# Reordered first loads, longer warm-up, paired first tiles and four output buffers in a gated two-branch attention kernel

## Chip, cores, metric

One core of one Trainium2 chip. The metric is the device time of one execution in microseconds (us); lower is better. The kernel ran alone on its core. The granted clock is the share of TensorE's full clock that a profile shows as granted.

## The reference

Two attention branches read the same x (2048 x 1024, bf16), and a sigmoid gate mixes their outputs:

```python
q, k, v = split_heads(x @ wqkv)                 # 32 heads of 32, in each branch with its own weights
# branch A: linear attention
kv, z = einsum(phi(k), v), sum_s(phi(k))        # phi(t) = max(t,0) + min(exp(t),1) + 1e-6
a = ((phi(q) @ kv) / (phi(q) . z)) @ wo_A
# branch B: softmax over 8 keys at a dilation of 2
b = (softmax(q . k[s - 2w] * scale) @ v[s - 2w]) @ wo_B
g = sigmoid((x * gate_w).sum(-1))
return g * a + (1 - g) * b
```

## The kernel before

TensorE goes through five stages: pk (phi of branch A's keys, with the weights WkA in two column halves), G (x^T pk), the values and branch A's queries, branch B's keys and queries with its attention (eight blocks of four heads, each attended while the next is projected), and the output projection. The change touches the beginning of pk and the attention blocks.

The first loads, and the x tiles. Tiles 0 and 1 of x are transposed on TensorE from a row-major copy; the other fourteen come through transposing DMAs on the sync queue, in order, with everything else behind them.

```python
    load_rows(nc.scalar, 0, 1)
    load_rows(nc.scalar, 1, 2)
    WkA = load_w("WkA", A_wqkv, D, "wa", parts=4, only=(0,))        # four DMAs of 256 KB, sync queue
    for t in range(2, NB):
        nc.sync.dma_start_transpose(out=xT[:, :, t * P:(t + 1) * P], in_=rows(x, t * P, (t + 1) * P))
    WkA += load_w("WkA", A_wqkv, D, "wa", only=(1,))
    # ... (cut) the other rows of x, other weights
            for i in range(5):
                warm = ps_1.tile([P, 512], F32, name="warm", tag="p1")
                for j in range(4):
                    nc.tensor.matmul(warm[:, j * P:(j + 1) * P], lhsT=onesb[:], rhs=onesb[:], start=True, stop=True)
            for t in range(2):
                # ... (cut) eight 128x128 transposes of xrow into tp
                nc.vector.tensor_copy(out=xT[:, 0:4, t * P:(t + 1) * P], in_=tp[:, 0:4, :])
                nc.scalar.copy(out=xT[:, 4:8, t * P:(t + 1) * P], in_=tp[:, 4:8, :])
            for half in range(2):
                for t in range(NB):
                    # ... (cut) pj = sum over kt of xT[:, kt, tile t] x WkA[half][:, kt, :]
                    phi(pk[:, t, half * 512:(half + 1) * 512], pj)
```

The output side of an attention group. `small` has two buffers; Ob holds the normalized output until a transposing DMA has read it:

```python
                    Ob = small.tile([P, 4, 4, Dh], BF16, name="Ob", tag="Ob")
                    # ... (cut) probabilities x V into PSUM banks oB
                        nc.vector.tensor_tensor(out=Ob[:, t0:t0 + m], in0=o_[:, :, :, 0:Dh],
                                                in1=rd[:, 0:m].broadcast_to([P, m, 4, Dh]), op=ALU.mult)
                        # ... (cut)
                        nc.sync.dma_start_transpose(out=OBT[:, c, ...], in_=Ob[0:w, t0:t0 + m]...)
    # before the last block is attended:
            WoB = load_w("WoB", B_wo, 0, "wb")
            nc.sync.dma_start_transpose(out=pqT[0][:], in_=pqd[0:512, :])
```

Of the kernel before, what the change touches and what calls it, by code (L numbers as in the profile page):

```python
# [10 lines left out]
BF16 = mybir.dt.bfloat16  # L11
F32 = mybir.dt.float32
PE = mybir.EngineType.PE
DVE = mybir.EngineType.DVE
P = 128
# [26 lines left out]
def kernel(  # L42
# [11 lines left out]
    nc = tc.nc  # L54
    S, D = A_x.shape[1:]
# [9 lines left out]
    Dh = D // H  # L65
    KT = D // P
    NB = S // P
# [8 lines left out]
    wpool = ctx.enter_context(tc.tile_pool(name="wpool", bufs=2))  # L76
# [2 lines left out]
    kq = ctx.enter_context(tc.tile_pool(name="kq", bufs=2))  # L79
    ps_pj = ctx.enter_context(tc.tile_pool(name="ps_pj", bufs=2, space=bass.MemoryType.PSUM))  # L80

    def load_w(name, src, col0, tag, parts=1, only=(0, 1)):
        halves = []
        for h in only:
            w = wpool.tile([P, KT, 512], BF16, name=f"{name}{h}", tag=tag)
            c0 = col0 + h * 512
            n = KT // parts
            for i in range(parts):
                nc.sync.dma_start(
                    out=w[:, i * n:(i + 1) * n, :],  # L90
                    in_=src[i * n * P:(i + 1) * n * P, c0:c0 + 512].rearrange("(kt p) n -> p kt n", p=P))
            halves.append(w)
        return halves

    xT = big.tile([P, KT, S], BF16, name="xT", tag="xT")
    xrow = big.tile([P, NB, D], BF16, name="xrow", tag="vV")

    def load_rows(eng, t0, t1):
        eng.dma_start(out=xrow[:, t0:t1, :], in_=rows(x, t0 * P, t1 * P).rearrange("(t p) d -> p t d", p=P))

    load_rows(nc.scalar, 0, 1)
    load_rows(nc.scalar, 1, 2)
    WkA = load_w("WkA", A_wqkv, D, "wa", parts=4, only=(0,))
    for t in range(2, NB):
        nc.sync.dma_start_transpose(out=xT[:, :, t * P:(t + 1) * P], in_=rows(x, t * P, (t + 1) * P))
    WkA += load_w("WkA", A_wqkv, D, "wa", only=(1,))
# [11 lines left out]
    onesb = consts.tile([P, P], BF16, name="onesb")  # L118
# [26 lines left out]
    def phi(dst, pj):  # L145
        e = work.tile([P, 512], F32, name="e", tag="e")
        nc.scalar.activation(out=e[:], in_=pj[:], func=ACT.Exp)  # L147
        nc.vector.tensor_scalar(out=e[:], in0=e[:], scalar1=1.0, scalar2=1e-6, op0=ALU.min, op1=ALU.add)  # L148
        nc.vector.scalar_tensor_tensor(out=dst, in0=pj[:], scalar=0.0, in1=e[:], op0=ALU.max, op1=ALU.add)

    with tc.manual_schedule(engines={PE}):

        with ExitStack() as s1:
# [1 line left out]
            junk = s1.enter_context(tc.tile_pool(name="junk", bufs=1))  # L155


            for i in range(5):
                warm = ps_1.tile([P, 512], F32, name="warm", tag="p1")
                for j in range(4):  # L160
                    nc.tensor.matmul(warm[:, j * P:(j + 1) * P], lhsT=onesb[:], rhs=onesb[:], start=True, stop=True)
            for t in range(2):
                tp = ps_1.tile([P, KT, P], BF16, name="xt_ps", tag="p1")
                for kt in range(KT):
                    nc.tensor.transpose(out=tp[:, kt, :], in_=xrow[:, t, kt * P:(kt + 1) * P], identity=ident[:])
                nc.vector.tensor_copy(out=xT[:, 0:4, t * P:(t + 1) * P], in_=tp[:, 0:4, :])
                nc.scalar.copy(out=xT[:, 4:8, t * P:(t + 1) * P], in_=tp[:, 4:8, :])

            s1.enter_context(tc.manual_schedule(engines={DVE}))
            pk = big.tile([P, NB, D], BF16, name="pk", tag="pkO")  # L170
            for half in range(2):
                for t in range(NB):
                    pj = ps_1.tile([P, 512], F32, name="pk_ps", tag="p1")
                    for kt in range(KT):
                        nc.tensor.matmul(pj[:], lhsT=xT[:, kt, t * P:(t + 1) * P], rhs=WkA[half][:, kt, :],  # L175
                                         start=(kt == 0), stop=(kt == KT - 1))
                    phi(pk[:, t, half * 512:(half + 1) * 512], pj)
            zacc = junk.tile([P, D], F32, name="zacc", tag="zacc")
            gw_row = junk.tile([P, D], BF16, name="gw_row", tag="gw")
            nc.gpsimd.dma_start(out=gw_row[:], in_=gate_w.partition_broadcast(P))  # L180
            zhl = junk.tile([P, 2, D], BF16, name="zhl", tag="zhl")

            def side(t):
# [133 lines left out]
        with ExitStack() as s2:  # L317
# [31 lines left out]
            def attention_events(c, kqt, cuts, first, lag):  # L349
                GROUPS = [QT[a:b] for a, b in zip(cuts, cuts[1:])]  # L350
                state = [dict() for _ in GROUPS]
                per_bank = 2 if cuts is CUTS4 else 3

                def scores(g):
                    tiles, st = GROUPS[g], state[g]
                    W_ = sum(w for _, w, _ in tiles)
                    s4 = ps_s.tile([P, 4, 512], F32, name="s4", tag="s")
                    o = 0
                    for q0, w, k0 in tiles:
                        for i in range(4):  # L360
                            r = slice(32 * i, 32 * i + 32)
                            nc.tensor.matmul(s4[:, i, o:o + w], lhsT=kqt[r, 0, k0:k0 + P],
                                             rhs=kqt[r, 1, q0:q0 + w], start=True, stop=True)
                        o += w
                    pt = PT[count[0] % 2]
                    count[0] += 1
                    ptv = pt[:, 0:4 * W_].rearrange("p (i s) -> p i s", i=4)
                    m0 = 112 if tiles[0][1] == 128 else 0 if tiles[1][1] == 128 else 240
                    for h in range(2):
                        hs = slice(2 * h, 2 * h + 2)  # L370
                        nc.scalar.activation(out=ptv[:, hs], in_=s4[:, hs, 0:W_], func=ACT.Exp, scale=SCALE)  # L371
                        m = mask[:, m0:m0 + W_]
                        nc.vector.tensor_tensor(out=ptv[:, hs], in0=ptv[:, hs],  # L373
                                                in1=m[:, None, :].broadcast_to([P, 2, W_]), op=ALU.mult)
                    st["pt"], st["W"] = pt, W_

                def pv(g):
                    tiles, st = GROUPS[g], state[g]
                    pt, W_, n = st["pt"], st["W"], len(tiles)
                    Ob = small.tile([P, 4, 4, Dh], BF16, name="Ob", tag="Ob")  # L380
                    oB = []
                    for b in range((n + per_bank - 1) // per_bank):
                        bank = ps_o.tile([P, 512], F32, name=f"oB{b}", tag=f"o{b}")
                        m = min(per_bank, n - per_bank * b)
                        oB.append((b * per_bank, m, bank[:, 0:m * 4 * (Dh + 1)].rearrange("p (t i e) -> p t i e", t=m, i=4)))
                    for t0, m, o_ in oB:
                        for i in range(4):
                            o = sum(w for _, w, _ in tiles[:t0])
                            for tt in range(t0, t0 + m):
                                nc.tensor.matmul(o_[:, tt - t0, i, :], lhsT=pt[:, i * W_ + o:i * W_ + o + P],  # L390
                                                 rhs=V[:, cuts[g] + tt, c * 4 + i, :], start=True, stop=True)
                                o += tiles[tt][1]
                    for t0, m, o_ in oB:
                        rd = small.tile([P, 3, 4, 1], F32, name="rd", tag="rd")
                        nc.vector.reciprocal(out=rd[:, 0:m], in_=o_[:, :, :, Dh:Dh + 1])
                        nc.vector.tensor_tensor(out=Ob[:, t0:t0 + m], in0=o_[:, :, :, 0:Dh],
                                                in1=rd[:, 0:m].broadcast_to([P, m, 4, Dh]), op=ALU.mult)
                    t0 = 0
                    while t0 < n:
                        q0, w, _ = tiles[t0]  # L400
                        m = 1
                        while t0 + m < n and tiles[t0 + m][1] == w and tiles[t0 + m][0] == q0 + m * w:
                            m += 1
                        nc.sync.dma_start_transpose(
                            out=OBT[:, c, q0:q0 + m * w].rearrange("p (t s) -> p t s", t=m),
                            in_=Ob[0:w, t0:t0 + m].rearrange("p t i e -> p (t i e)"))
                        t0 += m

                ev = []
                step = 64 / len(GROUPS)  # L410
                for g in range(len(GROUPS)):
                    ev.append((first + step * g, lambda g=g: scores(g)))
                    ev.append((first + step * g + lag, lambda g=g: pv(g)))
                return ev
# [12 lines left out]
            raw = wpool.tile([P, 4, D], BF16, name="raw", tag="wc")  # L427
            fw = wpool.tile([P, 2, D], F32, name="fw", tag="wc")
            pqT = [kq.tile([P, KT, 512], BF16, name="pqT0", tag="kq")]
            nc.sync.dma_start_transpose(out=pqT[0][:], in_=pqd[0:512, :])  # L430

            def qa_keep(t, half, pj):
                nc.scalar.copy(out=raw[:, t - 12, half * 512:(half + 1) * 512], in_=pj[:])
# [90 lines left out]
```

## Time and profile before

| | before |
|---|---|
| median of the first 3 runs | 496.87 us (496.01 to 497.5) |
| span of the profiled run | 493.9 us |
| TensorE busy | 481.6 us, 98% |

The page of the profiled run: the first line gives busy time, share of the span and number of instructions of TensorE (PE); the second is the chain of work that ended last, by engine.

```profile
PE 481.6 (98%) x3276; PEld 230.1 (47%) x3336; DVE 283.4 (57%) x550; ACT 182.0 (37%) x281; POOL 8.6 (2%) x29
...
PE 96%; DMA 2%; issue 1%; DVE 0%; ACT 0%; SPq 0%; ACTq 0%; DVEq 0%
```

TensorE is the bound, so a gain can come only from its idle time or its slow time. The timeline of TensorE's matmuls in the first 40 us (start, duration, engine, line, operation, out<-in, count, and in brackets the idle time before it and what ended it):

```profile
1.13 2.32 PE L161 MATMUL warm<-onesb 128*128 128x128 bf16 x20 [1.13 <-DVE onesb L119]
4.57 1.04 PE L165 MATMUL xt_ps<-ident,xrow 128*128 128x128 bf16 x8 [1.13 <-DMA xrow<-in_A_x_dram]
5.88 1.03 PE L165 MATMUL xt_ps<-ident,xrow 128*128 128x128 bf16 x8 [0.27 <-DMA xrow<-in_A_x_dram]
6.71 28.47 PE L175 MATMUL pk_ps<-WkA_77,xT 128*128 128x512 bf16 x125
35.01 5.34 PE L175 MATMUL pk_ps<-WkA_96,xT 128*128 128x512 bf16 x24
```

TensorE waits for x tile 0 and again for tile 1. The line at 35.01 is the first matmul with WkA's second half and serves as a clock: whatever happens at the start has been settled by then. The weight loads (PEld) in front of the first projection matmuls show the rate:

```profile
6.60 0.26 PEld L175 LDWEIGHTS <-xT 128*128 128x128 bf16 x2
7.14 0.15 PEld L175 LDWEIGHTS <-xT 128*128 128x128 bf16 x1 [0.28 <-issue]
7.56 0.15 PEld L175 LDWEIGHTS <-xT 128*128 128x128 bf16 x1 [0.28 <-issue]
7.99 4.03 PEld L175 LDWEIGHTS <-xT 128*128 128x128 bf16 x19 [0.28 <-ACT xT L167]
```

Single loads at 7.14, 7.56 and 7.99 mean 0.43 us for each 512-column matmul. From 7.99 on there are 19 loads in 4.03 us, about 0.216 us each: the array has changed to its full rate. The granted clock does not show this: it reads 1.00 in every stretch of the first 14 us, so the rate at the start is read from the distance of the weight loads.

In the last attention block (the sync queue, SPq in the view, with VectorE and TensorE; three views of the same run):

```profile
359.63 4.11 SPq L430 DMA_TRANSPOSE pqT_4069<-pqd  x1
...
365.13 1.60 SPq L89 DMA_DIRECT2D WoB_4065<-in_B_wo_dram  x1
366.83 14.76 SPq L404 DMA_TRANSPOSE OBT<-Ob  x8
```

```profile
367.71 0.56 DVE L396 TENSOR_TENSOR Ob<-oB_4153,rd 128x384 bf16<-128x384 f32 x1 [2.24 <-DMA OBT<-Ob]
...
372.44 0.56 DVE L396 TENSOR_TENSOR Ob<-oB_4202,rd 128x384 bf16<-128x384 f32 x1 [3.21 <-DMA OBT<-Ob]
```

```profile
PE oB_4252 L390 <- DVE Ob L396: 1.5, 1, 1.5
...
PE oB_4202 L390 <- DVE Ob L396: 0.5, 1, 0.5
```

VectorE cannot write Ob until an output transpose two groups back has read the buffer. That transpose sits on the queue behind the transpose of pqT0 (4.11 us of issue) and a 1 MB half of WoB. VectorE waits 2.24 and 3.21 us, and TensorE, which needs the PSUM bank that VectorE has not emptied, waits 0.50 and 1.51 us.

### The profile page before, as it was taken

To read this page: it belongs to the slowest core of one execution; us is meant where nothing else is said; L and a number is where in the kernel's file an instruction comes from. 1 tells how busy PE (TensorE), PEld (TensorE's weight loads), DVE (VectorE), ACT (ScalarE), POOL (GpSimd) and SP (SyncE) were. 2 spreads that over 40 slices of the span, in tenths; PEclk is the share of its full clock that TensorE was granted. 3 is DMA by queue.
4 is the path that set the end of the run, shared out by engine and by line. 5 is a ranking of instruction groups with operands and counts; after the bars stand their busy time and mean duration, and the time that the engine had idled before them with its cause. 6 is when DMAs were issued, how large, how long until landed. Compare 5 with 4: busy or idle time off the path is not lost.

```text
span 493.9 us, 8164 instructions
## 1 busy us (share of the span) xinstructions
PE 481.6 (98%) x3276; PEld 230.1 (47%) x3336; DVE 283.4 (57%) x550; ACT 182.0 (37%) x281; POOL 8.6 (2%) x29
## 2 busy tenths in 40 slices
PE   7999999999999999999999999999998999999997
PEld 4444444446444444444444444544444444444444
DVE  2666699921329999996567676767655596000000
ACT  2333311112543333331555655565564323112121
POOL 4000000001100000000000000000000000000000
PEclk9999999999999999999999999999999999999999
DMA  8999920002422122244011141111172843110101
GB/s 232 163 317 361 345 95 0 1 0 68 152 75 70 74 88 92 94 145 139 11 33 29 27 119 38 29 28 34 31 175 54 209 86 82 36 42 33 43 33 42
DMA packets 78069, 46.03 MB, mean 93 GB/s; under 512 B 51472, under 2 KB 72080, under 8 KB 78032
## 3 DMA queue, kind: packets, MB, share of 16 engines
q1 hardware_dynamic: 77664, 44.73, 32.9%
q10 hardware_dynamic: 288, 0.52, 0.4%
q8 instruction: 26, 0.43, 0.4%
q0 software_dynamic: 80, 0.26, 0.2%
q14 instruction: 11, 0.09, 0.1%
HBM read 21.23 MB, written 7.34 MB: 58 GB/s over the span
## 4 chain that ended last, share of the span: by engine, by line
PE 96%; DMA 2%; issue 1%; DVE 0%; ACT 0%; SPq 0%; ACTq 0%; DVEq 0%
PE kq_ps L334 22%; PE d_ps L452 21%; PE pk_ps L175 11%; PE g_ps L198 11%; PE p_ps L257 11%; PE p_ps L291 8%; PE q_ps L291 1%; DMA OBT<-Ob 1%; DMA xrow<-in_A_x_dram 1%; PE kv_ps L216 1%; PE q_ps_4367 L452 1%; PE p_ps L246 1%; PE q_ps L452 1%; PE q_ps_4147 L291 0%; PE q_ps_4248 L291 0%
## 5 line engine op out<-in xcount | busy, mean ns | idle before, releaser
L198 PE MATMUL g_ps<-pk,xrow 128*128 128x512 bf16 x251 | 55.2, 379 | 0.3
L457 ACT ACTIVATE osb<-d_ps,omg 128x512 bf16<-128x512 f32 (+1 forms) x31 | 20.9, 673 | 77.0 <-PE d_ps L452 72.5
L148 DVE TENSOR_SCALAR e<-e 128x512 f32<-128x512 f32 x64 | 27.2, 425 | 36.0 <-ACT e L147 35.8
L175 PEld LDWEIGHTS <-xT 128*128 128x128 bf16 x256 | 25.3, 99 | 30.4 <-issue 0.6
L452 PEld LDWEIGHTS <-OBT 128*128 128x128 bf16 x264 | 25.8, 98 | 29.2
L198 PEld LDWEIGHTS <-xrow 128*128 128x128 bf16 x256 | 25.0, 98 | 30.2
L257 PEld LDWEIGHTS <-xT 128*128 128x128 bf16 x256 | 25.0, 98 | 30.2
L291 PEld LDWEIGHTS <-xT 128*128 128x128 bf16 x256 | 24.2, 98 | 28.0
L373 DVE TENSOR_TENSOR PT_1878<-PT_1878,mask 128x672 bf16<-128x672 bf16 (+3 forms) x42 | 23.6, 571 | 17.0 <-ACT PT_1878 L371 16.7
L334 PE MATMUL kq_ps<-xT,WqB_1861 128*128 128x512 bf16 x120 | 31.8, 379 | 1.0 <-issue 0.6
L147 ACT ACTIVATE e<-pk_ps 128x512 f32<-128x512 f32 x32 | 19.1, 597 | 36.3 <-PE pk_ps L175 35.2
L334 PE MATMUL kq_ps<-xT,WqB_1859 128*128 128x512 bf16 x124 | 31.7, 379 | 0.7 <-issue 0.5
L334 PE MATMUL kq_ps<-xT,WkB_1056 128*128 128x512 bf16 x122 | 31.6, 379 | 0.2
L340 DVE CAST kqt<-kq_ps 128x512 bf16<-128x512 f32 x32 | 22.0, 687 | 16.4 <-PE kq_ps L334 16.4
L334 PE MATMUL kq_ps<-xT,WkB_1054 128*128 128x512 bf16 x120 | 30.7, 379 | 0.4 <-issue 0.2
L373 DVE TENSOR_TENSOR PT_1879<-PT_1879,mask 128x672 bf16<-128x672 bf16 (+3 forms) x40 | 22.2, 564 | 15.3 <-ACT PT_1879 L371 15.1
L257 PE MATMUL p_ps<-WvB_112,xT 128*128 128x512 bf16 x126 | 30.6, 379 | 0.1
L257 PE MATMUL p_ps<-WvB_110,xT 128*128 128x512 bf16 x125 | 30.6, 379 | 0.1
L262 ACT CAST tmp<-p_ps 128x512 bf16<-128x512 f32 x32 | 18.8, 587 | 30.3 <-PE p_ps L257 27.9
L452 PEld LDWEIGHTS <-pqT_4425 128*128 128x128 bf16 x200 | 19.6, 98 | 22.1
L175 PE MATMUL pk_ps<-WkA_77,xT 128*128 128x512 bf16 x125 | 28.3, 386 | 0.2
L452 PE MATMUL d_ps<-WoB_4065,OBT 128*128 128x512 bf16 (+1 forms) x126 | 28.3, 366 | 0.1
(400 smaller groups left out, 669.2 us busy)
## 6 DMA issues: line engine op xcount, KB each, us to landing
out_dram<-osb SPq DMA_DIRECT2D x31, 128.0 KB, 1.9
xrow<-in_A_x_dram SPq DMA_DIRECT2D x3, 1024.0 KB, 12.0
pqd<-tmp SPq DMA_DIRECT2D x12, 256.0 KB, 2.0
V<-tmp SPq DMA_DIRECT2D x4, 264.0 KB, 2.5
WkA_77<-in_A_wqkv_dram SPq DMA_DIRECT2D x4, 256.0 KB, 5.5
WkA_96<-in_A_wqkv_dram SPq DMA_DIRECT2D x1, 1024.0 KB, 7.0
WvA_102<-in_A_wqkv_dram SPq DMA_DIRECT2D x1, 1024.0 KB, 14.3
WvA_104<-in_A_wqkv_dram SPq DMA_DIRECT2D x1, 1024.0 KB, 15.2
```

The costliest lines, as they stand in the source:

```text
L147: nc.scalar.activation(out=e[:], in_=pj[:], func=ACT.Exp)
L148: nc.vector.tensor_scalar(out=e[:], in0=e[:], scalar1=1.0, scalar2=1e-6, op0=ALU.min, op1=ALU.add)
L175: nc.tensor.matmul(pj[:], lhsT=xT[:, kt, t * P:(t + 1) * P], rhs=WkA[half][:, kt, :], start=(kt == 0), stop=(kt == KT - 1))
L198: nc.tensor.matmul(pj[:], lhsT=xrow[:, t, kt * P:(kt + 1) * P], rhs=pk[:, t, half * 512:(half + 1) * 512], start=(t == 0), stop=(t == NB - 1))
L257: nc.tensor.matmul(st["pj"][:], lhsT=xT[:, kt, t * P:(t + 1) * P], rhs=WvB[half][:, kt, :], start=(kt == 0), stop=(kt == KT - 1))
L262: nc.scalar.copy(out=v[:, half * 16:(half + 1) * 16, 0:Dh], in_=st["pj"][:].rearrange("p (h e) -> p h e", h=16))
L291: nc.tensor.matmul(st["pj"][:], lhsT=xT[:, kt, t * P:(t + 1) * P], rhs=WqA[half][:, kt, :], start=(kt == 0), stop=(kt == KT - 1))
L334: nc.tensor.matmul(st["pj"][:], lhsT=W[c // 4][:, kt, (c % 4) * P:(c % 4 + 1) * P], rhs=xT[:, kt, cols], start=(kt == 0), stop=(kt == KT - 1))
L340: nc.vector.tensor_copy(out=kqt[:, 1, cols], in_=st["pj"][:])
L373: nc.vector.tensor_tensor(out=ptv[:, hs], in0=ptv[:, hs], in1=m[:, None, :].broadcast_to([P, 2, W_]), op=ALU.mult)
L452: nc.tensor.matmul(st["ps"][:, 0:n], lhsT=lhsT, rhs=W[c0 // 512][:, c, c0 % 512:c0 % 512 + n], start=(side == 0 and c == 0), stop=(side == ...
L457: nc.scalar.activation(out=osb[:, 0:n], in_=st["ps"][:, 0:n], func=ACT.Copy, scale=omg[:, tb:tb + 1])
```

## The change

Its intent: get both x tiles to the head of two queues, let weights follow in row blocks and use each block for two tiles, keep TensorE warm until data lands, move the gate row out of the crowded start, and give the attention output four buffers, so that VectorE can run ahead of the transposes of its output. pqT0 is cut in four. The order of instructions on VectorE stays the same.

```diff
-    load_rows(nc.scalar, 0, 1)
+    load_rows(nc.sync, 0, 1)
     load_rows(nc.scalar, 1, 2)
-    WkA = load_w("WkA", A_wqkv, D, "wa", parts=4, only=(0,))
+    WkA = [wpool.tile([P, KT, 512], BF16, name="WkA0", tag="wa")]
+    for kt in range(KT):
+        (nc.scalar if kt % 2 else nc.sync).dma_start(out=WkA[0][:, kt, :], in_=A_wqkv[kt * P:(kt + 1) * P, D:D + 512])
     # ... (cut)
-            for i in range(5):
-                warm = ps_1.tile([P, 512], F32, name="warm", tag="p1")
-                for j in range(4):
-                    nc.tensor.matmul(warm[:, j * P:(j + 1) * P], lhsT=onesb[:], rhs=onesb[:], start=True, stop=True)
+            def warm_up(n): ...                 # n matmuls of 128 columns into one PSUM tile (cut)
+            warm_up(28)
             for t in range(2):                  # the TensorE transposes (cut)
+            warm_up(6)
     # ... (cut)
-                for t in range(NB):
-                    pj = ps_1.tile([P, 512], F32, name="pk_ps", tag="p1")
+                for t0, n in [(0, 2)] + [(t, 1) for t in range(2, NB)]:
+                    pj = [ps_1.tile([P, 512], F32, name="pk_ps", tag="p1") for _ in range(n)]
                     for kt in range(KT):        # each weight block for all n tiles, then the next (cut)
     # ... (cut)
-            nc.gpsimd.dma_start(out=gw_row[:], in_=gate_w.partition_broadcast(P))
+            nc.sync.dma_start(out=gw_row[:], in_=gate_w.partition_broadcast(P))
     # ... (cut)
-                    Ob = small.tile([P, 4, 4, Dh], BF16, name="Ob", tag="Ob")
+                    Ob = small.tile([P, 4, 4, Dh], BF16, name="Ob", tag="Ob", bufs=4)
     # ... (cut)
-            nc.sync.dma_start_transpose(out=pqT[0][:], in_=pqd[0:512, :])
+            for t in range(4):
+                nc.sync.dma_start_transpose(out=pqT[0][:, :, t * P:(t + 1) * P], in_=pqd[t * P:(t + 1) * P, :])
```

More of the change, by code (lines that the diff above doesn't have):

```diff
@@ L80, with load_w @@
     ps_pj = ctx.enter_context(tc.tile_pool(name="ps_pj", bufs=2, space=bass.MemoryType.PSUM))
-    def load_w(name, src, col0, tag, parts=1, only=(0, 1)):
+    def load_w(name, src, col0, tag, only=(0, 1)):
         halves = []
@@ L86, in load_w @@
             c0 = col0 + h * 512
-            n = KT // parts
-            for i in range(parts):
-                nc.sync.dma_start(
-                    out=w[:, i * n:(i + 1) * n, :],
-                    in_=src[i * n * P:(i + 1) * n * P, c0:c0 + 512].rearrange("(kt p) n -> p kt n", p=P))
+            nc.sync.dma_start(out=w[:], in_=src[:, c0:c0 + 512].rearrange("(kt p) n -> p kt n", p=P))
             halves.append(w)
@@ L155, with warm_up @@
             junk = s1.enter_context(tc.tile_pool(name="junk", bufs=1))
-            for i in range(5):
-                warm = ps_1.tile([P, 512], F32, name="warm", tag="p1")
-                for j in range(4):
-                    nc.tensor.matmul(warm[:, j * P:(j + 1) * P], lhsT=onesb[:], rhs=onesb[:], start=True, stop=True)
+            def warm_up(n):
+                warm = ps_1.tile([P, P], F32, name="warm", tag="p1")
+                for i in range(n):
+                    nc.tensor.matmul(warm[:], lhsT=onesb[:], rhs=onesb[:], start=True, stop=True)
+            warm_up(28)
             for t in range(2):
@@ L171 @@
             for half in range(2):
-                for t in range(NB):
-                    pj = ps_1.tile([P, 512], F32, name="pk_ps", tag="p1")
+                for t0, n in [(0, 2)] + [(t, 1) for t in range(2, NB)]:
+                    pj = [ps_1.tile([P, 512], F32, name="pk_ps", tag="p1") for _ in range(n)]
                     for kt in range(KT):
-                        nc.tensor.matmul(pj[:], lhsT=xT[:, kt, t * P:(t + 1) * P], rhs=WkA[half][:, kt, :],
-                                         start=(kt == 0), stop=(kt == KT - 1))
-                    phi(pk[:, t, half * 512:(half + 1) * 512], pj)
+                        for i in range(n):
+                            t = t0 + i
+                            nc.tensor.matmul(pj[i][:], lhsT=xT[:, kt, t * P:(t + 1) * P], rhs=WkA[half][:, kt, :],
+                                             start=(kt == 0), stop=(kt == KT - 1))
+                    for i in range(n):
+                        phi(pk[:, t0 + i, half * 512:(half + 1) * 512], pj[i])
             zacc = junk.tile([P, D], F32, name="zacc", tag="zacc")
             gw_row = junk.tile([P, D], BF16, name="gw_row", tag="gw")
-            nc.gpsimd.dma_start(out=gw_row[:], in_=gate_w.partition_broadcast(P))
+            nc.sync.dma_start(out=gw_row[:], in_=gate_w.partition_broadcast(P))
             zhl = junk.tile([P, 2, D], BF16, name="zhl", tag="zhl")
```

## The prediction

> TensorE bounds the kernel from end to end. The page gives PE 481.6 us busy in a span of 493.9 (98%), and the chain that ended last is PE for 96%. Full-rate matmuls take 216 ns (8 in 1.73 us). So the change can gain only where PE idles or runs slowly: at most about 12 us.
>
> **Start.** In the timeline, 20 warm-up matmuls run from 1.13 to 3.45 us (116 ns each); PE then waits 1.12 us for the first x tile (transposes at 4.57) and 0.27 us for the second (5.88). The first projection group begins at 6.71, but its weight loads at 7.14, 7.56 and 7.99 are 0.42 us apart, half the later rate. The projection's second half starts at 35.01; less 128 matmuls of 216 ns and a few 0.05 us gaps, the stage behaves as if started at full rate at 7.3 us. The Trainium skill, "TensorE: Matmul & The Clock Gate", Part 1, says that the array starts at half rate and is released by a busy window of about 3.4 us, free-running. The trace agrees: after the idle microsecond before 4.57, half rate lasts until about 8.0. The granted-clock row does not show it.
>
> The change puts two tiles at the head of two queues. By the table of stretches 0.52 MB has moved by 4.15 us; I expect both tiles at about 4.5 (today 4.5 and 5.83). 28 warm-ups last until about 4.4, so PE has no gap and should reach full rate near 4.6 to 6. The 16 transposes then take 1.1 to 1.9 us (today 1.03 per eight); with a 0.42 us copy the paired groups start near 6.0 to 6.9. Pairing gives each 128 KB weight block 0.43 us of PE work; estimated to land between 5.5 and 8.0, they should keep just ahead. Gain: 1.2 us (0.3 to 1.7).
>
> The gate row leaves the start: 0.26 MB off busy DMA engines. It comes at about 55 us, for use at 66, where VectorE has slack. The added issue on SP delays the x transposes by under 0.5 us; tile 2 is needed at about 9.5 and should land by 8.5. WkA's second half landed at 33.0 and will be needed at 33.7: tight, but the gate row's absence (about 0.9 us of traffic) pays for it.
>
> **Last attention block.** In the chain, an output transpose issued at 366.83 lands after 5.52 us (median 2.3), behind a 1 MB WoB half (issued 365.13, 6.7 us) and the pqT0 transpose (4.11 us of issue). With two Ob buffers VectorE waits 2.24 and 3.21 us for those transposes, and PE then 0.50 and 1.51 us for the PSUM bank. Four buffers, with groups 3 us apart, give 6 us more patience: both PE waits, 2.0 us, go. The split pqT0 costs about 6.6 us of issue (1.65 each, as xT shows) and delays output transposes by some 2.5 us, within that patience; its first quarter is there well before 377. Elsewhere VectorE never waits for Ob: no gain there.
>
> **Sum.** 496.87 - 1.2 - 2.0 = 493.7 us; range 492.2 to 495.3. Chances: faster by over 2% 0.01, within 2% 0.98, slower 0.01.
>
> Shown right by: no PE wait for xrow over 0.3 us; the projection's second half starting at about 33.8; no 0.42 us steps in the first groups; no wait on Ob. Wrong if: weight blocks land late and the pair stalls; tile 2 or WkA's second half comes late; the gate opens late; or the four pqT0 transposes delay the output transposes so far that Ob waits return.

## The result

| | before | after |
|---|---|---|
| median | 496.21 us (6 runs, 495.44 to 497.5) | 493.85 us (6 runs, 493.06 to 494.99) |
| ratio, with 95% interval | | 0.9952 (0.9933 to 0.9971) |
| span of the profiled run | 493.9 us | 493.0 us |

Ratios are the mean time of one kernel's fast runs over that of the other's of the same rounds, so not quite the ratio of the medians quoted. 0.9952 of 496.4 is a gain of 2.4 us. The predicted time, 493.7, was met within 0.2 us, but it had been reached from 496.87, so the predicted gain was 3.2 us. Which of its parts came?

The page of after, the same two lines:

```profile
PE 487.6 (99%) x3350; PEld 232.0 (47%) x3350; DVE 283.3 (57%) x550; ACT 181.9 (37%) x281; POOL 7.9 (2%) x28
...
PE 98%; DMA 1%; ACT 0%; issue 0%; ACTq 0%
```

TensorE is now 99% busy, and its busy time has gone up by 6 us; part of that is slow matmuls and part matmul records that the trace of before lacks (3276 against 3350 recorded, with only 14 more in the program). Busy time is no gain here. The timeline of TensorE in the first 40 us:

```profile
1.12 3.17 PE L159 MATMUL warm<-onesb 128*128 128x128 bf16 x28 [1.12 <-DVE onesb L117]
5.19 1.89 PE L165 MATMUL xt_ps<-ident,xrow 128*128 128x128 bf16 x16 [0.91 <-DMA xrow<-in_A_x_dram]
...
7.51 29.21 PE L178 MATMUL pk_ps<-WkA_77,xT 128*128 128x512 bf16 x128
36.56 3.62 PE L178 MATMUL pk_ps<-WkA_100,xT 128*128 128x512 bf16 x16
```

The clock line with WkA's second half has moved from 35.01 to 36.56: **the new start was 1.55 us slower** in the profiled run. The x tiles came at 5.14, not 4.5, so that TensorE idled 0.91 us after its 28 warm-ups. The weight loads:

```profile
7.41 0.29 PEld L178 LDWEIGHTS <-xT 128*128 128x128 bf16 x2
7.94 0.15 PEld L178 LDWEIGHTS <-xT 128*128 128x128 bf16 x1 [0.24 <-issue]
8.37 0.15 PEld L178 LDWEIGHTS <-xT 128*128 128x128 bf16 x1 [0.27 <-issue]
...
10.07 0.15 PEld L178 LDWEIGHTS <-xT 128*128 128x128 bf16 x1 [0.27 <-issue]
10.45 1.61 PEld L178 LDWEIGHTS <-xT 128*128 128x128 bf16 x8 [0.22 <-issue]
```

Full rate began only near 10.4, 2.4 us later than in the run of before. The sync queue, which should have issued the first transposing DMA for x at about 3.2, and the scalar queue (ACTq), which should have issued its last weight block before 3:

```profile
1.26 1.84 SPq L101 DMA_DIRECT2D WkA_77<-in_A_wqkv_dram  x4
5.16 6.81 SPq L103 DMA_TRANSPOSE xT<-in_A_x_dram  x4
```

```profile
1.25 5.43 ACTq L101 DMA_DIRECT2D WkA_77<-in_A_wqkv_dram  x4
```

```profile
SPq L103 <- DMA xrow<-in_A_x_dram: 2.0, 1, 2.0
```

The four weight DMAs of the scalar queue took from 1.25 to 6.68 us to issue, and the sync queue stood 2.0 us waiting for an x load. The compiled program's own list of waits tells why: DMAs from the two hardware queues take eight completion semaphores (the counters by which the program learns that a DMA is done) in turn, and a DMA is issued only when the one that used its semaphore before has completed. Before, six loads stood at the start (two x, four weights); now there are ten, and three of the DMAs at the start wait for a load eight places ahead of them: the first x transpose, and the scalar queue's last two loads, which are WkA's row blocks 5 and 7.

The last attention block went as foreseen. In the list of TensorE's waits only the start is left (the whole answer), and VectorE no longer waits for Ob anywhere:

```profile
PE warm L159 <- DVE onesb L117: 1.1, 1, 1.1
PE xt_ps L165 <- DMA xrow<-in_A_x_dram: 0.9, 1, 0.9
```

```profile
361.18 1.25 SPq L436 DMA_TRANSPOSE pqT_4084<-pqd  x1
...
364.41 6.75 SPq L436 DMA_TRANSPOSE pqT_4084<-pqd  x3
371.25 11.23 SPq L409 DMA_TRANSPOSE OBT<-Ob  x8
```

The four pieces of pqT0 take 8.0 us to issue (1.25 + 6.75) where the one transpose took 4.11, more than the predicted 6.6, and the output transposes behind them leave later than before. Nobody waits for them.

What was this worth? The first output copy of the output projection on ScalarE marks the end of the attention blocks (before, then after):

```profile
383.42 0.69 ACT L457 ACTIVATE osb<-q_ps_4367,omg 128x512 bf16<-128x512 f32 x1 [3.17 <-PE q_ps_4367 L452]
```

```profile
382.61 0.69 ACT L463 ACTIVATE osb<-q_ps_4385,omg 128x512 bf16<-128x512 f32 x1 [3.17 <-PE q_ps_4385 L458]
```

That is 0.81 us earlier although the stage started 1.55 us late, so the last block gained 0.81 + 1.55 = 2.36 us. I compared ScalarE's instructions of the two traces one by one: the offset is 1.55 us from the second projection group to the last attention block and -0.81 us from there to the end. Apart from the tiles that are now paired and some copies that changed places in the output stage, nothing else in the kernel moved.

From this came two theories. **A:** the whole gain is the four Ob buffers; the new start is worth nothing on average, because its gain is taken back by the late x tiles, the later full rate and the late weight blocks. **B**, the prediction's view: the start is worth 1.2 us on average, and the profiled run merely caught full rate beginning late.

### The profile page after: what moved, and what is told of

The parts are those of the page before. It is cut to its first block, busy times and chain, and to the rows that moved or that the text cites. A ratio compares the mean times of both kernels' runs of the same rounds, so it can differ in the third digit from the quotient of the medians.

```text
span 493.0 us, 8254 instructions
## 1 busy us (share of the span) xinstructions
PE 487.6 (99%) x3350; PEld 232.0 (47%) x3350; DVE 283.3 (57%) x550; ACT 181.9 (37%) x281; POOL 7.9 (2%) x28
## 4 chain that ended last, share of the span: by engine, by line
PE 98%; DMA 1%; ACT 0%; issue 0%; ACTq 0%
PE kq_ps L339 23%; PE d_ps L458 21%; PE pk_ps L178 11%; PE p_ps L262 11%; PE g_ps L203 11%; PE p_ps L296 8%; PE q_ps L296 2%; DMA xrow<-in_A_x_dram 1%; PE kv_ps L221 1%; PE q_ps_4385 L458 1%; PE q_ps L458 1%; PE p_ps L251 1%; PE xt_ps L165 0%; PE q_ps_4266 L296 0%; PE q_ps_4165 L296 0%; PE z_ps L228 0%
## 5 line engine op out<-in xcount | busy, mean ns | idle before, releaser
L339 PE MATMUL kq_ps<-xT,WkB_1071 128*128 128x512 bf16 x128 | 32.9, 380 | 0.0
L339 PE MATMUL kq_ps<-xT,WqB_1876 128*128 128x512 bf16 x128 | 32.9, 379 | 0.0
L339 PE MATMUL kq_ps<-xT,WkB_1069 128*128 128x512 bf16 x128 | 32.3, 379 | 0.0
L339 PE MATMUL kq_ps<-xT,WqB_1874 128*128 128x512 bf16 x128 | 32.2, 379 | 0.0
```

The lines of the kernel that those rows point to most:

```text
L339: nc.tensor.matmul(st["pj"][:], lhsT=W[c // 4][:, kt, (c % 4) * P:(c % 4 + 1) * P], rhs=xT[:, kt, cols], start=(kt == 0), stop=(kt == KT - 1))
```

## The experiments

All twelve gave correct results. Two marks place each profile: the start of ScalarE's first copy of G (mark 1; 66.29 us before, 67.84 after), which carries the start's whole effect, and the first output copy shown above (mark 2). Their distance was 317.13 us before and 314.77 after.

| label | what | median us (runs) | ratio to before (95%) | mark 1 | mark 2 - mark 1 |
|---|---|---|---|---|---|
| e1_ob_only | before + four Ob buffers | 494.32 (6) | 0.9950 (0.9932 to 0.9967) | 67.57 | 314.77 |
| e2_start_only | the new start alone | 496.09 (6) | 0.9986 (0.9969 to 1.0003) | 66.19 | 316.67 |
| e3_split_only | pqT0 in four alone | 498.71 (6) | 1.0041 (1.0022 to 1.0059) | 67.88 | 319.29 |
| e4_six_loads | after, WkA in 4 blocks | 494.32 (6) | 0.9948 (0.9928 to 0.9967) | 67.42 | 314.76 |
| e5_warm36 | after, 36 warm-ups | 494.10 (6) | 0.9957 (0.9938 to 0.9976) | 66.59 | 314.77 |
| e6_warm0 | after, no warm-ups ahead of x | 494.57 (6) | 0.9969 (0.9948 to 0.9989) | 67.15 | 314.77 |
| e7_old_start_bridged | e1 with 29 warm-ups | 493.07 (6) | 0.9942 (0.9922 to 0.9962) | 66.11 | 314.77 |
| e8_both_halves | both WkA halves per tile | 493.11 (6) | 0.9936 (0.9918 to 0.9954) | 66.46 | 314.77 |
| e9_tiles_2_3_first | e8, tiles 2, 3 ahead | 493.06 (5) | 0.9941 (0.9928 to 0.9954) | 65.75 | 314.77 |
| e10_six_warm36 | after, 4 blocks and 36 warm-ups | **492.16** (5) | **0.9923** (0.9909 to 0.9936) | 66.09 | 314.77 |
| e11_after_again | after | 494.43 (5) | 0.9962 (0.9948 to 0.9975) | 67.34 | 314.77 |
| e12_ob_only_again | e1 once more | 493.60 (5) | 0.9956 (0.9943 to 0.9970) | 66.51 | 314.76 |

The first four, the next four and the last four each shared a chip and the runs of before.

### The parts of the change

**Four Ob buffers alone.**

```diff
-Ob = small.tile([P, 4, 4, Dh], BF16, name="Ob", tag="Ob")
+Ob = small.tile([P, 4, 4, Dh], BF16, name="Ob", tag="Ob", bufs=4)
```

> The kernel before with four Ob buffers and nothing else. Theory A (the whole measured gain, about 2.4 us, is the Ob buffers, and the new start is worth nothing on average): 2.0 to 2.5 us faster than before, both PE waits on Ob (0.50 and 1.51 us) and both VectorE waits (2.24 and 3.21 us) gone. Theory B (my prediction: start 1.2, Ob 2.0, and the profiled run of after merely had a bad start): 2.0 us faster, and the rest of the gain shows in the start-only run.

Measured: 0.9950, about 2.5 us, with the marks' distance 2.36 us shorter. The Ob waits of both engines are gone. The old start in this run was no better than the new one (mark 1 at 67.57): the beginning of full rate varies for it too.

**The new start alone** (after, with Ob at two buffers and pqT0 whole).

```diff
-                    Ob = small.tile([P, 4, 4, Dh], BF16, name="Ob", tag="Ob", bufs=4)
+                    Ob = small.tile([P, 4, 4, Dh], BF16, name="Ob", tag="Ob")
-            for t in range(4):
-                nc.sync.dma_start_transpose(out=pqT[0][:, :, t * P:(t + 1) * P], in_=pqd[t * P:(t + 1) * P, :])
+            nc.sync.dma_start_transpose(out=pqT[0][:], in_=pqd[0:512, :])
```

> The changed kernel with Ob back at two buffers and pqT0 as one transpose: the new start and the moved gate row alone. Theory A: within 0.5 us of before; the x tiles land at about 5.1 us, the first transpose into xT is issued at about 5.2 (it waits for the first x load, which holds the completion semaphore that it reuses), WkA's second half lands at about 34.7 and its first matmul starts between 34.7 and 36.6, depending on when the array's full rate begins. Theory B: 1.2 us faster than before, first matmul of the second half at about 33.8 in a usual run.

Measured: 0.9986, about 0.7 us, with an interval that holds zero (and 1.2 us as well). In its profiled run, the fastest of the six (494.73), half a microsecond was not from the start: mark 1 was 0.10 us earlier than before, while two Ob waits happened to be shorter (316.67). In this profile full rate had come early; yet TensorE then waited 0.4 us for WkA, where the changed kernel's profiled run had no such wait. Early full rate does not help when the weight blocks are not there.

**pqT0 in four alone.**

```diff
-nc.sync.dma_start_transpose(out=pqT[0][:], in_=pqd[0:512, :])
+for t in range(4):
+    nc.sync.dma_start_transpose(out=pqT[0][:, :, t * P:(t + 1) * P], in_=pqd[t * P:(t + 1) * P, :])
```

> The kernel before with pqT0 cut in four and two Ob buffers. If the pieces only add issue time on the queue (about 2.5 us, as predicted), the output transposes behind them come later, VectorE waits longer for Ob and PE's waits there grow from 2.0 to 3 us or more: slower than before by 1 to 2.5 us. If, as a rival, the pieces help by letting an output transpose and the WoB half go between them, the waits shrink and the time falls by up to 2 us.

Measured: slower by 2.0 us, in the upper half of the first expectation; the rival falls. TensorE waits 2.8 us at once for VectorE's Ob:

```profile
372.18 0.47 PE L390 MATMUL oB<-V,PT 128*128 128x33 bf16 x12 [2.77 <-DVE Ob L396]
```

And more follows. Stretches of the same profile (from:to, length, then busy us and count of PE, PEld, DVE, ACT and POOL, then PEclk, DMA share, GB/s):

```profile
369.00:372.00 3.00, 0.41 (x2) 0.00 (x0) 0.43 (x1) 0.41 (x1) 0.00 (x0) 1.00 0.96 109
372.00:373.00 1.00, 0.82 (x14) 0.51 (x15) 1.00 (x4) 0.09 (x1) 0.00 (x0) 0.89 1.06 239
373.00:374.00 1.00, 1.00 (x3) 0.15 (x1) 0.10 (x1) 0.50 (x1) 0.00 (x0) 0.50 1.15 195
...
375.00:376.00 1.00, 1.00 (x4) 0.30 (x3) 0.89 (x2) 0.99 (x2) 0.00 (x0) 0.50 0.14 28
376.00:378.00 2.00, 1.94 (x19) 0.92 (x18) 1.19 (x4) 0.59 (x1) 0.00 (x0) 0.95 0.34 70
```

The granted clock falls to 0.50 right after the wait and stays there for more than 3 us. That one followed from the other is argued from this order in one profile. The sizes fit: the waits grew by 0.76 us (2.77 against 0.50 + 1.51), and some 3.4 us at half clock (from the granted clock of the stretches) cost an estimated 1.7 us, together a little over the 2.16 us by which the marks moved apart (319.29 against 317.13). So the expectation was met in size, but most of the loss came from the clock, which it did not name. The other runs fit too: the one with a granted clock of 1.000 took 497.10 us, the five with 0.995 to 0.997 took 498.43 to 499.40. With four buffers (after against e1: 314.77 both) the split costs and gains nothing.

**After and Ob-only again, side by side** (both kernels unedited).

> The changed kernel once more, on the same chip as four Ob buffers alone. Theory A (start worth nothing on average): ratio to before 0.995, within 0.1% of the Ob-only run beside it. Theory B (start worth 1.2 us): 0.25% faster than it.

> The kernel before with four Ob buffers alone, once more. Theory A: 2.3 to 2.5 us under before, and within 0.5 us of the changed kernel beside it. Theory B: 1.2 us slower than the changed kernel.

Measured: 0.9962 and 0.9956. The small difference, 0.06%, is against the new start; each ratio is good to about 0.13%, so their difference to some 0.19%, and a gain of 1.2 us would be 0.24%. A gain of up to about 0.7 us is not excluded, 1.2 us is. The profiles agree: mark 1 is 67.06 on average with the old start (before, e1, e3, e12) and 67.12 with the new (after, e2, e11), and in both it varies by about 1.6 us. Theory A holds for the value; the next runs ask for its cause.

### Why the start gained nothing

**Six early loads instead of ten.**

```diff
-    for kt in range(KT):
-        (nc.scalar if kt % 2 else nc.sync).dma_start(out=WkA[0][:, kt, :], in_=...[kt * P:(kt + 1) * P, D:D + 512])
+    for i in range(4):                          # 256 KB each, two per queue
+        (nc.scalar if i % 2 else nc.sync).dma_start(out=WkA[0][:, 2 * i:2 * i + 2, :], in_=...)
```

> The changed kernel with WkA's first half in four blocks of 256 KB, two on each queue, so that only six loads stand ahead of the x transposes and none reuses a semaphore. If that reuse is what cancels the start's gain: the first xT transpose is issued at about 2.2 us instead of 5.2, WkA's second half lands at about 32.5 to 33.3 instead of 34.7, and the kernel is 0.5 to 1 us faster than the changed one. If the start is set by the x tiles' landing and by when full rate begins: x tiles still land at 5.0 or later (more traffic competes), the second half's first matmul starts at 34.5 to 36.6 as before, and the time is within 0.5 us of the changed kernel.

Measured: 0.9948, equal to after. The first x transpose was issued at 2.23 as expected, but WkA's second half landed no earlier (issued 28.04, 7.1 us to landing), which was a miss: the fourteen x transposes took as much longer. Full rate began late in this profile (near 9.5), so late blocks would not have shown. One of its six runs took 492.10 us, the level that e10 reaches below; it was not profiled.

**36 warm-ups instead of 28.**

```diff
-            warm_up(28)
+            warm_up(36)
```

> The changed kernel with 36 warm-up matmuls ahead of the transposes instead of 28, to end at about 5.3 us at 116 ns each, just when the x tiles land (5.1 to 5.3 in the three profiles of the new start). If the idle 0.9 us between warm-ups and x tiles is what delays full rate in most executions (it began at 10.4 in the profile of the changed kernel, at 4.3 in the start-only one): no wait of PE for xrow, full rate begins between 4.5 and 8 us in every execution, the second half's first matmul at 34.7 to 35.5, and the time is 0.5 to 1 us under the changed kernel's with less spread. If the gap does not matter, or other waits (WkA blocks 5 and 7, WkA's second half at 34.7) take the gain back: within 0.3 us of the changed kernel.

Measured: 0.9957, equal to after: the second branch. TensorE did not wait for xrow, and full rate came near 6.6 us; but TensorE then waited for WkA (0.4 us listed, 0.65 us on its weight load). In this profile blocks 5 and 7 took part of the time won back (mark 1 is 66.59, against 66.09 with both edits in e10 below). In all four profiles with 36 warm-ups (e5, e8, e9, e10) full rate was there when the projection began, between 6.4 and 7.1 us; with 28 it was in two of four (e2, e11; e4 and after reached it near 9.5 and 10.4). That is suggestive, not proof.

**No warm-ups ahead of x.**

```diff
-            warm_up(28)
```

> The changed kernel without the 28 warm-ups ahead of the transposes. If the warm-ups, with the gap behind them, seldom bring full rate forward: PE starts at about 5.2, full rate begins between 8.6 and 12 us as in most executions of the changed kernel, and the time is within 0.4 us of it. If they do their work on average (prediction): 1 us or more slower than the changed kernel.

Measured: 0.9969, some 0.6 us slower than 36 warm-ups beside it and 0.3 to 0.8 us slower than after in its two runs, with overlapping intervals. Not the 1 us or more of the prediction, but also not proof of nothing: this one stays open. Its profile had full rate at 8.2, a little earlier than expected.

**Both together: six loads and 36 warm-ups.**

```diff
-            warm_up(28)
+            warm_up(36)
 # and the four 256 KB blocks of e4
```

> The changed kernel with six early loads and 36 warm-ups together. With 36 warm-ups alone full rate began at 6.65 us, but PE then waited for WkA row blocks 5 and 7, which the scalar queue had issued only after the first loads had landed (0.4 us wait and 0.65 us of idle weight load). If the reused semaphore is the cause: no PE wait for WkA here, second half's first matmul about 0.5 to 0.9 us earlier than with 36 warm-ups alone at a like start of full rate, time 0.4 to 0.8 us under the changed kernel. If the weights are late because of the traffic as such: the wait stays, though all blocks are issued by 2.5 us.

Measured: 0.9923, with an interval that lies wholly below that of after on the same chip. This is larger than expected (1.9 us under after). The two profiles pair well, because full rate begins at nearly the same time in both. TensorE's matmuls, first of the changed kernel (e11), then with both edits (e10):

```profile
1.12 3.17 PE L159 MATMUL warm<-onesb 128*128 128x128 bf16 x28 [1.12 <-DVE onesb L117]
4.94 1.82 PE L165 MATMUL xt_ps<-ident,xrow 128*128 128x128 bf16 x16 [0.65 <-POOL mask L127]
...
6.93 0.38 PE L178 MATMUL pk_ps<-WkA,xT 128*128 128x512 bf16 x1
7.51 1.89 PE L178 MATMUL pk_ps<-WkA,xT 128*128 128x512 bf16 x8 [0.20 <-issue]
10.60 3.61 PE L178 MATMUL pk_ps<-WkA,xT 128*128 128x512 bf16 x16 [1.20 <-DMA WkA<-in_A_wqkv_dram]
```

```profile
1.12 4.02 PE L161 MATMUL warm<-onesb 128*128 128x128 bf16 x36 [1.12 <-DVE onesb L119]
5.12 1.75 PE L167 MATMUL xt_ps<-ident,xrow 128*128 128x128 bf16 x16
...
7.04 0.38 PE L180 MATMUL pk_ps<-WkA,xT 128*128 128x512 bf16 x1
7.62 6.64 PE L180 MATMUL pk_ps<-WkA,xT 128*128 128x512 bf16 x30 [0.20 <-issue]
```

In e11 eight recorded matmuls are followed by a wait of 1.20 us for WkA, until 10.60; in e10 they run through. (The 0.65 us at 4.94 that the view puts down to POOL is the wait for the x tile; the weight load in front of it is listed as waiting for xrow. Wait lists name the releaser that came last by the profile.) Mark 1 is at 67.34 and 66.09: 1.25 us, the size of that wait. The scalar queue's weight blocks, in e11 and in e10:

```profile
1.25 5.20 ACTq L101 DMA_DIRECT2D WkA<-in_A_wqkv_dram  x4
```

```profile
1.25 1.00 ACTq L101 DMA_DIRECT2D WkA<-in_A_wqkv_dram  x2
```

The late blocks went with their late issue; that traffic as such made them late, the rival named in the expectation, falls. (That the blocks of e10 are also twice as large was not tested apart.)

So there were two obstacles in series. When full rate comes late, the slow matmuls hide the late weight blocks; when it comes early, the weight blocks show. Removing one shows no gain clear of the noise (e4 0.9948, e5 0.9957, after 0.9952 and 0.9962); removing both does. The pair of profiles shows the second obstacle directly. For the first the evidence is thinner: e4 and e5 ran on other chips, and while the interval of e10 lies below that of e5, it overlaps that of e4 (0.9928 to 0.9967), which lacks only the eight warm-ups.

### Other starts

**The old start with four Ob buffers and 29 warm-ups.**

```diff
-            for i in range(5):
+            for i in range(6):
                 warm = ...
-                for j in range(4):
+                for j in range(4 + (i > 0) * 1):        # 4 + 5 * 5 = 29 matmuls
 # and Ob with bufs=4
```

> The kernel before with four Ob buffers and 29 warm-ups instead of 20 (to about 4.5 us, when the first x tile lands there): the old order of loads with the gap before the first tile closed; 0.3 to 0.8 us remain before the second tile. If the gap is what matters and not the order of loads: 0.5 to 1 us faster than four Ob buffers alone, so about 3 us faster than before, and not slower than the changed kernel with 36 warm-ups. If the new order of loads is needed for it: no faster than four Ob buffers alone (2.5 us under before).

Measured: 0.9942, about 2.9 us, close to the expected 3. By the ratios that is 0.4 to 0.7 us better than the two runs of Ob alone, but the intervals overlap. Its six loads never met the semaphore limit, so closing most of the gap was the only edit it needed; its profile shows two waits for xrow of 0.3 us. With these intervals it can't be ranked against e10.

**Both WkA halves for each tile, six loads, 36 warm-ups.**

```diff
+    WkA.append(wpool.tile([P, KT, 512], BF16, name="WkA1", tag="wa"))
+    for i, q in enumerate((nc.sync, nc.scalar)):            # 512 KB on each queue, ahead of the x transposes
+        q.dma_start(out=WkA[1][:, 4 * i:4 * i + 4, :], in_=...)
     for t in range(2, NB):                                  # the x transposes
-    WkA += load_w("WkA", A_wqkv, D, "wa", only=(1,))
     # ... (cut)
-            for half in range(2):
-                for t0, n in [(0, 2)] + [(t, 1) for t in range(2, NB)]:
+            for t0, n in [(0, 2)] + [(t, 1) for t in range(2, NB)]:
+                for half in range(2):
 # and the edits of e10
```

> A try at the best version: six early loads, 36 warm-ups, and both column halves of WkA loaded ahead of the x transposes and used for each x tile in turn, so that x tiles are needed every 3.45 us instead of 1.73 and WkA's second half is not behind fourteen transposes. If WkA's second half (landing at 33 to 35 us) caps the start's gain: no cap is left, the first G matmul starts 0.5 to 1 us earlier than with 36 warm-ups alone, and the kernel is 3.3 to 4.3 us under before. If the cap does not bind in most executions: equal to the 36 warm-ups version within 0.4 us. Risk: with 2.5 MB ahead of it, WkA's second half is late for the pair at about 10.4 us, which would show as PE waits on it of up to 1 us.

Measured: 0.9936, about 3.2 us, just short of the 3.3 to 4.3 expected; mark 1 was only 0.13 us earlier than in e5. The six runs lie within 0.32 us (492.91 to 493.23), where those of after spread over 1.9. The risk named came true: TensorE waited for WkA's second half near 10 us (1.2 us on the weight load). My reading is that all executions end up at this one wait, whenever full rate begins; that is argued from the spread, not tested further.

**Tiles 2 and 3 ahead of WkA's second half.**

```diff
+    for t in (2, 3): ...                                    # x transposes ahead of WkA's second half (cut)
     # ... (cut) WkA's second half, as in e8
-    for t in range(2, NB):
+    for t in range(4, NB):
     # ... (cut)
-            for t0, n in [(0, 2)] + [(t, 1) for t in range(2, NB)]:
-                for half in range(2):
+            for t0, n, halves in ([(0, 2, (0,)), (2, 1, (0,)), (3, 1, (0,))] + [(t, 1, (1,)) for t in range(4)]
+                                  + [(t, 1, (0, 1)) for t in range(4, NB)]):
+                for half in halves:
```

> The version that uses both halves of WkA per x tile, with x tiles 2 and 3 transposed in ahead of WkA's second half, and tiles 0 to 3 taken through the first half before the second. In the former version PE waited 1.2 us near 10 us for WkA's second half; here it is needed at about 13.8 us. If that wait is all that stood between the early full rate and the stage's end: no wait of PE over 0.3 us after the x tiles, first G matmul 0.7 to 1.2 us earlier than with both halves at once (in an execution whose full rate begins before 8 us), time 0.4 to 1 us under it, with some spread back, because the moment at which full rate begins shows again. If data stays the limit: a new wait for x tile 2 or for the weights, and the same time within 0.3 us.

Measured: 0.9941, no faster than e8 (493.06 against 493.11 us): the second expectation, data stays the limit. Its profile had the earliest mark 1 of all (65.75), but the runs spread again (492.54 to 493.7), and a weight load waited 0.56 us for an x tile. The simpler e10 has the lowest ratio of all versions that were run, though the intervals of e7, e8 and e9 overlap with its own.

## Why the prediction was right or wrong

The predicted time was right; of the two terms that it was summed from, one was a little small and the other did not come.

- **Last block, predicted 2.0 us, measured 2.36** (e1, and every other profile with four buffers to 0.01 us). The mechanism was right, the term a little small. The list of waits counts idle time from a matmul's end as drawn, 379 ns after its start, while successors start 216 ns apart. A wait also exposes that tail. My estimate from these numbers: 0.50 + 1.51 + 2 x 0.163 = 2.34 us.
- **Split pqT0 "within that patience": right.** It costs nothing with four buffers, and 2.0 us without them (e3).
- **Start, predicted 1.2 us, measured none that is clear of the noise** (e11 against e12; e2). Three steps failed. First, "I expect both tiles at about 4.5": they came 4.9 to 5.4 us after the start in all profiles of the new order. I had taken the moment when 0.52 MB had moved. Weights follow on the same two queues; in the run of after, some 0.84 MB had moved by 5.14 (the sum of the stretches). That the weights slow the tiles is argued only. So TensorE did have a gap, and full rate began late in some executions. The gap alone does not decide it: it was 1.01 us in e2, where the transposes at 5.30 already ran at full rate (16 in 1.07 us, against 1.89 in after). The Trainium skill, "TensorE: Matmul & The Clock Gate", Part 1, says that the window is free-running, so that the moment varies by execution; one and the same kernel reached full rate near 10.4 us in after and 6.6 in e11, and the old start near 10.3 in e1 and 8.5 in e12.
- Second, "they should keep just ahead" failed: blocks 5 and 7 were late whenever full rate came early (0.4 us in e2 and e5, 1.2 in e11). I had read the order of DMAs on each queue, but not the waits that the compiled program puts before them. The Trainium skill, "DMA: Bandwidth & Descriptors", in the section "Anatomy of one DMA — SWDGE (gpsimd) path", says that a semaphore wait happens on the issuing sequencer, before the DMA is dispatched; the trace agrees: the scalar queue took 5.43 us to issue four blocks, and 1.00 us for two in e10.
- Third, "The added issue on SP delays the x transposes by under 0.5 us": the first was issued at 5.16 instead of 2.87, by the same cause. WkA's second half landed later too, at about 34.7 instead of 33.0, which TensorE did not have to wait for in the profiled run; that the first delay caused this is not shown, since in e4 the first transpose was issued at 2.23 and the half still landed at about 35.1.
- The gain was there to be had: with 36 warm-ups and six loads the new start (e10) is about 1.6 us faster than four Ob buffers alone on the same chip (0.9923 against 0.9956, good to about 1 us).
- **No loss elsewhere: right.** The moved gate row cost nothing, and from the second group of pk to the last attention block all instructions of ScalarE kept one offset.

That a sum of one term too small and one that was not there came within 0.2 us was luck in part: it owes something to the first three runs of before, whose median (496.87) lay 0.7 us over that of all six (496.21).

## What to carry to other kernels

Count the DMAs that are in flight before the first data is used: where completion semaphores are handed out in turn, one load more than there are semaphores turns into a wait for the first of them, on the queue, with everything behind it. Bridge the time until data lands with warm-up matmuls that end after the data, not shortly before it, and do not expect either remedy to show its worth alone when two obstacles stand in series. Where a consumer's buffers are released by DMAs on a queue that also carries megabyte loads, give it as many buffers as the longest such load spans, since a TensorE wait of some 3 us can be paid twice, as in e3.

## What the Trainium skill lacked or had wrong

- "TensorE: Matmul & The Clock Gate": warns against TensorE idling for more than about 3 us between bursts, and names a window of 3.4 us. Here a single listed wait of 2.8 us was followed by a granted clock of 0.50 for over 3 us (e3), so a wait a little under either figure is not safe; this rests on one profile. The page also gives no measure of how much idle time a warm-up window may hold, and here the gap alone did not decide: with 0.91 us the first full rate came near 10.4 us (after), with 0.93 near 9.5 (e4), with 0.65 at about 6.6 (e11), and with 1.01 it was there by 5.3 (e2).
- "DMA: Bandwidth & Descriptors": has nothing on the cost of completion semaphores used in turn. Ten early loads on eight semaphores held the scalar queue's last weight block until 6.2 us and the first x transpose until 5.16 (2.23 with six loads).
